# Three large loads merged into one DMA each over 128 partitions, and a list scheduler given measured durations

## The chip, the cores and the metric

The kernel runs on one core of one Trainium2 chip. The metric is the device time of one execution in microseconds (us). An execution is classed as slow when it takes over 1.5% more than the fastest of the same kernel.

Two words are used throughout. A *DMA engine* is one of the 16 units (the profile's page counts 16 for the core) that move data between HBM and the core's memory (SBUF). A *semaphore* is the counter that a load raises when its data has landed. The trace records these raises, and so shows when each load landed. The engines stand under short names in the views: TensorE (PE; PEld for its weight loads) does the matmuls, VectorE (DVE), ScalarE (ACT) and GpSimd (POOL) the rest of the arithmetic, and SyncE (SP) issues the loads. The span is the time from a program's first to its last instruction.

## The reference

Two layers are applied twice: a gated long convolution (A) and a small MLP (B), on a sequence of 2048 rows of 512.

```python
def _A_ref(q, k, v, shift_k, ssm_k, ssm_D):
    k_shift = sum over 4 taps of (k moved by t rows) * shift_k[:, tap]
    kv = k_shift * v
    y  = long convolution of kv with ssm_k (by FFT over 2*S) + kv * ssm_D
    return q * y
def _B_ref(x, w1, b1, w2, b2):
    return gelu(layernorm(x) @ w1 + b1) @ w2 + b2
# cut: types, padding, the FFT calls
x = A_q
x = x + _A_ref(layernorm(x), A_k, A_v, ...);  x = x + _B_ref(layernorm(x), ...)
x = x + _A_ref(layernorm(x), A_k, A_v, ...);  x = x + _B_ref(layernorm(x), ...)
```

The convolution result y does not depend on q. So the kernel computes y once, from k and v. Then it loads q, and the two layers follow.

## The kernel before

The program is built in three steps. Each operation is recorded with its reads, writes and an assumed duration. A list scheduler chooses engine and order from those durations. Then semaphore waits are put in. Every engine is given its own list, in that order.

```python
# P.op(engines, function, duration in ns, reads, writes, ...) records one operation
def dma(dst, src, nbytes, reads=(), prio=0.0, writes=None):          # all loads go through SyncE's queue
    return P.op(SP, lambda e: e.dma_start(dst, src, allow_slow_non_contiguous=True), 550.0, reads=reads,
                writes=[dst] if writes is None else writes, dma=True, nbytes=nbytes, prio=prio)
# A(p0, n, off, dims): n partitions of SBUF from p0;  dr(tensor, off, dims): HBM, dims = [step, count]
# ... cut: small tables, ssm_k (4 loads), shift_k
dma(A(64, 64, R_K, [1, 1536]), dr(A_k, 13 * 512, [32 * 512, 64], [1, 1536]), 3 << 16)     # three rows of halo
dma(A(1, 63, R_K, [1, 1536]), dr(A_k, 29 * 512, [32 * 512, 63], [1, 1536]), 3 << 16)
for g in range(2):
    dma(A(64 * g, 64, R_K + 1536, [1, 8192]), dr(A_k, 16 * g * 512, [32 * 512, 64], [1, 8192]), 1 << 20)
for g in range(2):
    dma(A(64 * g, 64, R_V, [1, 8192]), dr(A_v, 16 * g * 512, [32 * 512, 64], [1, 8192]), 1 << 20)
for j in range(8):
    tload(t_s2, 64 * 384, j * 3072, R_S2 + j * 3072, 3072)           # 6 MB of DFT tables, 128 partitions
# ... cut: transforms of ssm_k (PE, ACT)
def shift_chunk(w):                                                  # VectorE: taps of k, then times v
    # ... cut: three taps, adds, fourth tap, adds (7 operations of 128x2048)
    tt(..., A(0, 128, R_V + ...), ALU.mult, 610.0)                   # the first use of v, twice
    stage1(R_KP, ...)                                                # PE: first transform of kv
for w in range(4): shift_chunk(w)
products(0); products(1)                                             # VectorE: spectra times ssm_k's
inverse1(0); inverse1(1)
for g in range(2):                                                   # q, into memory that the spectra leave
    dma(A(64 * g, 64, R_X, [1, 8192]), dr(A_q, 16 * g * 512, [32 * 512, 64], [1, 8192]), 1 << 20)
# ... cut: second table, w1, w2, biases, then per layer and block: statistics of x, norms, MLP, residual
```

Partition p = 64g + c holds 16 consecutive rows of 512 from row 32c + 16g on. Each partition's data is one row of 16 KB in HBM. The 64 partitions of one half g take every second 16 KB row.

Of the kernel before, what the change touches and what calls it, by code (L numbers as in the profile page):

```python
# [7 lines left out]
ALU = mybir.AluOpType  # L8
AF = mybir.ActivationFunctionType
# [405 lines left out]
def bass_interleave_layers__ssm_conv_h3__mixer_channel_mlp__prompt_kernel(  # L415
        nc, A_q, A_k, A_v, A_shift_k, A_ssm_k, A_ssm_D, B_x, B_w1, B_b1, B_w2, B_b2, out):
    P = Prog(nc)
# [71 lines left out]
    dma(A(0, 128, R_SR, [1, 2048]), dr(A_shift_k, 0, [0, 128], [1, 2048]), 1 << 19)  # L489
    dma(A(64, 64, R_K, [1, 1536]), dr(A_k, 13 * 512, [32 * 512, 64], [1, 1536]), 3 << 16)  # L490
    dma(A(1, 63, R_K, [1, 1536]), dr(A_k, 29 * 512, [32 * 512, 63], [1, 1536]), 3 << 16)
    for g in range(2):
        dma(A(64 * g, 64, R_K + 1536, [1, 8192]), dr(A_k, 16 * g * 512, [32 * 512, 64], [1, 8192]), 1 << 20)
    for g in range(2):
        dma(A(64 * g, 64, R_V, [1, 8192]), dr(A_v, 16 * g * 512, [32 * 512, 64], [1, 8192]), 1 << 20)
    for j in range(8):
        tload(t_s2, 64 * 384, j * 3072, R_S2 + j * 3072, 3072)

# [9 lines left out]
    for a4 in range(4):  # L508
        tl = Tile(dconv)
        for al in range(4):  # L510
            ins = []
            for b in range(4):
                for g in range(2):
                    src = A(0, 128, R_HRAW + b * 2048 + 16 * g + 4 * a4 + al, [32, 64])
                    ins.append((g, al * 512 + b * 128, src))

            def f(e, ins=ins, tl=tl):
                for g, o, src in ins:
                    r = e.transpose(QB(tl, 64 * g, 64, o, [1, 128]), src, IDN)
                return r  # L520
            P.op(PE, f, 8 * 60.0, reads=[x[2] for x in ins] + [IDN], tile=tl)
        dst = A(0, 128, R_HP + 16 * a4, [4, 4], [64, 128], [1, 4])

        def f(e, dst=dst, tl=tl):
            src = QB(tl, 0, 128, 0, [512, 4], [4, 128], [1, 4])
            if e is nc.scalar:
                return e.activation(dst, src, AF.Copy)
            return e.tensor_copy(dst, src)
        P.op((ACT, DVE), f, {ACT: 2048 * .833 + 60, DVE: 2048 * .52 + 70}, writes=[dst], tile=tl)

    def stage1(src, G, gk, gh, dg0, n, engs, prio=0.0):


        for d8 in range(dg0 // 8, (dg0 + n) // 8):
            for h in range(2):
                tl = Tile(dconv)
                ins = [(64 * g, i, A(64 * g, 64, src + (64 * h + 8 * d8 + i) * 64, [1, 64]), A(64 * g, 64, R_F, [1, 128]))
                       for i in range(8) for g in range(2)]

                def f(e, ins=ins, tl=tl):  # L540
                    for p, i, w, m in ins:
                        r = e.matmul(Q(tl, p, 64, i * 128, [1, 128]), w, m, start=True, stop=True)  # L542
                    return r
                P.op(PE, f, 16 * 45.0, reads=[x for y in ins for x in y[2:]], tile=tl, prio=prio)
                dst = A(0, 128, G + gh(h, 8 * d8), [gk, 128], [1, 8])

                def f(e, dst=dst, tl=tl):
                    src = Q(tl, 0, 128, 0, [1, 128], [128, 8])
                    if e is nc.scalar:
                        return e.activation(dst, src, AF.Copy)  # L550
                    return e.tensor_copy(dst, src)
                P.op(engs, f, {ACT: 1100.0, DVE: 1024 * 1.04 + 90}, writes=[dst], tile=tl, prio=prio)

    def stage2(G, ks, n, pool, prio=0.0):

# [18 lines left out]
    for k4 in range(16):  # L574
        tl = stage2(R_GH, range(4 * k4, 4 * k4 + 4), 128, dconv, HP)
        dst = A(0, 128, R_H + k4 * 1024, [1, 1024])

        def f(e, dst=dst, tl=tl):
            src = Q(tl, 0, 128, 0, [1, 1024])
            if e is nc.scalar:  # L580
                return e.activation(dst, src, AF.Copy)  # L581
            return e.tensor_copy(dst, src)
        P.op((ACT, DVE), f, {ACT: 1024 * .833 + 60, DVE: 1024 * 1.04 + 70}, writes=[dst], tile=tl, prio=HP)


    def tt(o, a, b, op, dur, eng=DVE):
# [7 lines left out]
    def shift_chunk(w):  # L594

        tm = [A(0, 128, R_KP + w * 1024, [64, 16], [4096, 2], [1, 64])]
        tm += [A(0, 128, o, [128, 16], [64, 2], [1, 64]) for o in (R_TMP, R_TMP + 2048)]

        def tap(j, o):

            tt(o, A(0, 128, R_K + (3 - j) * 512 + w * 64, [512, 16], [256, 2], [1, 64]),
               A(0, 128, R_SJ[w] + j * 128, [0, 16], [64, 2], [1, 64]), ALU.mult, 1140.0)
        for j in range(3):
            tap(3 - j, tm[j])
        tt(tm[1], tm[0], tm[1], ALU.add, 1140.0)
        tap(0, tm[0])
        tt(tm[2], tm[1], tm[2], ALU.add, 1140.0)
        tt(tm[1], tm[2], tm[0], ALU.add, 1140.0)
        for h in range(2):
            tt(A(0, 128, R_KP + (64 * h + 16 * w) * 64, [4, 16], [64, 16], [1, 4]),  # L610
               A(0, 128, R_TMP + 64 * h, [128, 16], [4, 16], [1, 4]),
               A(0, 128, R_V + 256 * h + w * 64, [512, 16], [4, 16], [1, 4]), ALU.mult, 610.0)
        stage1(R_KP, R_GX + 8192 * (w // 2), 64, lambda h, dg: 32 * h + dg % 32, 16 * w, 16, EV_X)

    nx = [0]
# [1 line left out]
    def products(hf):  # L617

        for k8 in range(8):
# [5 lines left out]

            def f(e, xb=xb, tl=tl):
                return e.activation(xb, Q(tl, 0, 128, 0, [1, 1024]), AF.Copy)  # L627
            P.op(ACT, f, 1024 * .833 + 60, writes=[xb], tile=tl)
            ho = R_H + k8 * 2048 + 64 * hf
            x3 = A(0, 128, xo, [128, 8], [64, 2], [1, 64])  # L630
            tt(A(0, 128, po, [128, 8], [64, 2], [1, 64]), x3, A(0, 128, ho, [256, 8], [128, 2], [1, 64]), ALU.mult, 600.0)
            tt(x3, x3, A(0, 128, ho + 128, [256, 8], [-128, 2], [1, 64]), ALU.mult, 600.0)
            for ri, p in ((0, po), (1, xo)):
                tt(A(0, 128, R_Y + ri * 8192 + 8 * k8 * 64 + 32 * hf, [64, 8], [4096, 2], [1, 32]),
                   A(0, 128, p, [128, 8], [32, 2], [1, 32]), A(0, 128, p + 64, [128, 8], [32, 2], [1, 32]),
                   ALU.add if ri else ALU.subtract, 330.0)

    def inverse1(hf):

        for d4 in range(8 * hf, 8 * hf + 8):  # L640
# [14 lines left out]
            def f(e, dst=dst, tl=tl):  # L655
# [1 line left out]
                if e is nc.scalar:  # L657
                    return e.activation(dst, src, AF.Copy)  # L658
                return e.tensor_copy(dst, src)
            P.op((ACT, DVE), f, {ACT: 1024 * .833 + 60, DVE: 1024 * 1.04 + 70}, writes=[dst], tile=tl)  # L660

    for w in range(4):
        shift_chunk(w)
# [5 lines left out]


    tload(t_sm, row, 768, R_T2, 4096)
    for g in range(2):
        dma(A(64 * g, 64, R_X, [1, 8192]), dr(A_q, 16 * g * 512, [32 * 512, 64], [1, 8192]), 1 << 20)
    dma(A(0, 128, R_W1, [1376, 4], [1, 1376]), dr(B_w1, 0, [1376, 128], [128 * 1376, 4], [1, 1376]), 1409024)
    dma(A(0, 128, R_W2, [512, 10], [1, 512]), dr(B_w2, 0, [512, 128], [128 * 512, 10], [1, 512]), 1310720)
    dma(A(0, 96, R_W2 + 5120, [1, 512]), dr(B_w2, 1280 * 512, [512, 96], [1, 512]), 98304)
# [13 lines left out]
    for al2 in range(8):  # L690
# [18 lines left out]
        def f(e, dst=dst, tl=tl):  # L709
# [1 line left out]
            if e is nc.scalar:  # L711
                return e.activation(dst, src, AF.Copy)
            return e.tensor_copy(dst, src)
        P.op((ACT, DVE), f, {ACT: 1024 * .833 + 60, DVE: 1024 * 1.04 + 70}, writes=[dst], tile=tl)


    ptr, pm1, pm2 = Pool(1, 2), Pool(1, 3), Pool(1, 3)
# [2 lines left out]
    def stats(sl, double):  # L720
# [5 lines left out]
        for i, s in enumerate(sl):  # L726
            st = M(0, 128, M_ST + 6 * (4 * k + i), [1, 6])
            x = A(0, 128, R_X + s * 512, [1, 512])
            P.op(DVE, lambda e, st=st, x=x: e.bn_stats(st, x), 600.0, reads=[x], writes=[st])  # L729
            o = M(0, 128, mv + 2 * i, [1, 2])  # L730
            P.op(DVE, lambda e, st=st, o=o: e.bn_aggr(o, st), 100.0, reads=[st], writes=[o])
        v = M(0, 128, mv + 1, [2, n])
        r = M(0, 128, M_RS + 4 * k, [1, n])
        m1, a1 = (1.0 + EPS, EPS * EPS) if double else (1.0, EPS)
        P.op(POOL, lambda e: e.tensor_scalar(v, v, m1, a1, ALU.mult, ALU.add), 200.0, reads=[v], writes=[v])
        hf = M(0, 128, M_HF, [1, n])
        P.op(POOL, lambda e: e.tensor_tensor(r, v, hf, ALU.pow), 400.0, reads=[v, hf], writes=[r])  # L737
        return [(M(0, 128, mv + 2 * i, [1, 1]), M(0, 128, M_RS + 4 * k + i, [1, 1])) for i in range(n)]

    def norm(s, mr, o):  # L740
        x = A(0, 128, R_X + s * 512, [1, 512])
        m, r = mr
        P.op(DVE, lambda e: e.tensor_scalar(o, x, m, r, ALU.subtract, ALU.mult), 260.0, reads=[x, m, r], writes=[o])  # L743

    nn = [0]

# [6 lines left out]
    for L in range(2):  # L753
        for b in range(4):
            sl = list(range(4 * b, 4 * b + 4))
            mr = stats(sl, False)
            for i, s in enumerate(sl):
# [1 line left out]
                zt = A(0, 128, z, [1, 512])  # L759
                x = A(0, 128, R_X + s * 512, [1, 512])  # L760
                norm(s, mr[i], zt)
                tt(zt, zt, A(0, 128, R_YT + s * 512, [1, 512]), ALU.mult, 340.0)
                tt(x, x, zt, ALU.add, 340.0)
            mr = stats(sl, True)
            k = blk[0] % 2
            blk[0] += 1
            for i, s in enumerate(sl):
# [12 lines left out]
                def f(e, dst=dst, tl=tl):  # L780
# [1 line left out]
                    if e is nc.scalar:  # L782
                        return e.activation(dst, q, AF.Copy)  # L783
                    return e.tensor_copy(dst, q)
                P.op((ACT, DVE), f, {ACT: 490.0, DVE: 340.0}, writes=[dst], tile=tl)
            for fc in range(11):
                rows = 128 if fc < 10 else 96
                tl = Tile(pm1)
# [3 lines left out]
                def f(e, ins=ins, tl=tl, rows=rows):  # L792
# [4 lines left out]
                dst = A(0, rows, R_HT + k * 5632 + fc * 512, [1, 512])  # L797
                bias = M(0, rows, M_B1 + fc, [1, 1])
                P.op(ACT, lambda e, dst=dst, tl=tl, rows=rows, bias=bias: e.activation(  # L799
                    dst, Q(tl, 0, rows, 0, [1, 512]), AF.Gelu_apprx_tanh, bias=bias), 580.0,  # L800
                    reads=[bias], writes=[dst], tile=tl)
            for i, s in enumerate(sl):
                tl = Tile(pm2)
# [5 lines left out]
                for lo, hi in ((0, 4), (4, 8), (8, 11)):  # L809
                    def f(e, ins=ins, tl=tl, lo=lo, hi=hi):  # L810
# [2 lines left out]
                        return r  # L813
                    P.op(PE, f, (hi - lo) * 216.0, reads=[x for y in ins[lo:hi] for x in y], tile=tl)
                x = A(0, 128, R_X + s * 512, [1, 512])
                P.op(DVE, lambda e, x=x, tl=tl: e.tensor_tensor(x, x, Q(tl, 0, 128, 0, [1, 512]), ALU.add), 610.0,  # L816
                     reads=[x], writes=[x], tile=tl)
            if L == 1:
                for g in range(2):
# [34 lines left out]
```

## Time and profile before

| | before |
|---|---|
| time, median of 3 runs | 301.05 us (300.64 to 302.83) |
| span of the profiled run | 298.7 us |
| k landed / v landed / q landed | 24.0 / 34.6 / 93.8 us |
| first VectorE operation on k / on v | 24.07 / 35.43 us |

The landings are the last raises of each load's semaphore in the trace.

These are two lines from the part of the profile's page that follows the chain of work that ended last: shares of the span by engine, then by line.

```profile
PE 57%; DVE 20%; DMA 9%; ACT 7%; SPq 2%; POOL 2%; issue 1%
PE ps L794 25%; PE ps L812 24%; DVE ar L587 14%; DMA ar<-in_A_v_dram 9%; DVE sm L729 2%; PE ps L775 2%; ACT ar L658 2%; PE ps L566 2%; ACT ar L581 2%; SPq L470 2%; ACT ar L627 1%; POOL sm L737 1%; DVE ar L816 1%; ACT ar L550 1%; PE ps L650 1%
```

L794 and L812 are the MLP's matmuls, the second half of the kernel. Ahead of them stand VectorE (DVE), whose shift chunks and products are L587, and the load of v. The next view, of one source line, says when the MLP runs. The line is the weight loads of L794; the two times after the durations are the first and the last start.

```profile
L794 PEld LDWEIGHTS ps<-ar x352: 95/98/151, 131.1 to 273.8; 128*128 128x128 bf16 x160, 128*96 128x96 bf16 x16
```

VectorE's timeline (start, length, operation, count, and in brackets the idle time before it and what ended it):

```profile
15.85 2.38 DVE L528 COPY ar<-ps 128x2048 bf16<-128x2048 bf16 x2 [2.75 <-PE ps L519]
24.07 38.17 DVE L587 TENSOR_TENSOR ar<-ar 128x2048 bf16<-128x2048 bf16 x36 [5.84 <-DMA ar<-in_A_k_dram]
...
102.33 1.28 DVE L729 BATCH_NORM_STATS2 sm<-ar 128x6 f32<-128x512 bf16 x2
```

VectorE waits 5.84 us for k and then works through 36 operations without a pause. The single operations in the trace show that the eleventh, at 35.43 us, is the first that reads v, 0.8 us after v has landed. The layer-norm statistics of q start at 102.33 us, when q has been there for 8 us.

SyncE's queue, which issues the loads (start, time until the last of the group was issued):

```profile
4.38 2.32 SPq L470 DMA_DIRECT2D ar<-in_A_k_dram  x4
6.74 1.25 SPq L470 DMA_DIRECT2D ar<-in_A_v_dram  x2
8.03 10.84 SPq L478 DMA_DIRECT2D ar<-tab_s  x8
...
79.77 1.27 SPq L470 DMA_DIRECT2D ar<-in_A_q_dram  x2
```

The busy times in two stretches follow. The last three columns are the granted TensorE clock, the mean busy share of the 16 DMA engines, and the rate in GB/s. The engines come first in each row, with the count of instructions in brackets.

```profile
core 0: us, PE busy (x) PEld busy (x) DVE busy (x) ACT busy (x) POOL busy (x), PEclk, DMA share, GB/s
15.00:30.00 15.00, 10.23 (x232) 9.12 (x229) 8.31 (x8) 12.56 (x12) 0.00 (x0) 0.89 1.00 210
36.00:48.00 12.00, 8.87 (x192) 7.18 (x192) 11.83 (x13) 10.10 (x11) 0.00 (x0) 0.81 1.02 416
```

The first stretch carries k and v in halves of 64 partitions, the second the tables over 128. All engines are busy in both, but in the first they move half as much. A 16 KB row took about 1.25 us there. A 6 KB row of the tables took 0.236 us, at which rate 16 KB would take 0.63.

### The profile page before, as it was taken

The numbers are of one execution on the slowest core, as the hardware profiler recorded it, in microseconds if no ns is written. First come the engines' busy times: TensorE is split into PE (matmuls) and PEld (weight loads), VectorE is DVE, ScalarE is ACT, GpSimd is POOL, SyncE is SP. The second block draws the span as 40 slices with busy tenths as digits, with TensorE's granted clock in tenths as the row PEclk, the third lists the DMA queues.
The fourth block names the chain that finished last, engine by engine and source line by source line (L and its number), as shares of the span: only waits on it lengthen the run. The fifth ranks groups of instructions, "written<-read, shape, count | busy, mean of one in ns | idle before, by whom it ended". The sixth has DMA issues, their size and how long they took to land.

```text
span 298.7 us, 5389 instructions
## 1 busy us (share of the span) xinstructions
PE 247.2 (83%) x2304; PEld 145.5 (49%) x2304; DVE 194.8 (65%) x409; ACT 153.8 (51%) x196; POOL 25.7 (9%) x43
## 2 busy tenths in 40 slices
PE   0667175899899386169999999999999999999993
PEld 0666155788889284133444534444434444434441
DVE  0137999989999999899687775866995111201132
ACT  1069097689968299245445264454468502373100
POOL 2000000300010031213011011030021000000000
PEclk9989779799999899669999999999999999999998
DMA  6999996000199600000000000000000000200222
GB/s 203 295 211 211 278 414 214 2 20 3 37 224 324 193 27 2 1 2 0 0 2 0 0 1 2 0 0 2 0 0 3 0 0 2 70 0 0 72 70 70
DMA packets 7473, 22.10 MB, mean 74 GB/s; under 512 B 2490, under 2 KB 4123, under 8 KB 6938
## 3 DMA queue, kind: packets, MB, share of 16 engines
q1 hardware_dynamic: 7450, 21.76, 25.7%
q8 instruction: 18, 0.29, 0.4%
q14 instruction: 5, 0.04, 0.0%
HBM read 19.66 MB, written 2.10 MB: 73 GB/s over the span
## 4 chain that ended last, share of the span: by engine, by line
PE 57%; DVE 20%; DMA 9%; ACT 7%; SPq 2%; POOL 2%; issue 1%
PE ps L794 25%; PE ps L812 24%; DVE ar L587 14%; DMA ar<-in_A_v_dram 9%; DVE sm L729 2%; PE ps L775 2%; ACT ar L658 2%; PE ps L566 2%; ACT ar L581 2%; SPq L470 2%; ACT ar L627 1%; POOL sm L737 1%; DVE ar L816 1%; ACT ar L550 1%; PE ps L650 1%
## 5 line engine op out<-in xcount | busy, mean ns | idle before, releaser
L587 DVE TENSOR_TENSOR ar<-ar 128x512 bf16<-128x512 bf16 (+2 forms) x164 | 92.7, 620 | 7.2 <-DMA ar<-in_A_k_dram 5.8
L799 ACT ACTIVATE ar<-ps,sm 128x512 bf16<-128x512 f32 (+1 forms) x88 | 59.4, 687 | 53.0 <-PE ps L794 29.3
L794 PE MATMUL ps<-ar 128*128 128x512 bf16 (+1 forms) x352 | 82.4, 383 | 0.0
L812 PE MATMUL ps<-ar 128*128 128x512 bf16 (+1 forms) x352 | 79.6, 379 | 0.0
L794 PEld LDWEIGHTS ps<-ar 128*128 128x128 bf16 (+1 forms) x352 | 31.1, 101 | 46.8 <-ACT ar L799 17.8
L812 PEld LDWEIGHTS ps<-ar 128*128 128x128 bf16 (+1 forms) x352 | 33.2, 98 | 40.5 <-ACT ar L799 3.2
L816 DVE TENSOR_TENSOR ar<-ar,ps 128x512 bf16<-128x512 bf16 x32 | 21.0, 682 | 47.4 <-PE ps L812 47.4
L729 DVE BATCH_NORM_STATS2 sm<-ar 128x6 f32<-128x512 bf16 x64 | 41.8, 681 | 0.4
L743 DVE TENSOR_SCALAR ar<-ar,sm 128x512 bf16<-128x512 bf16 x64 | 23.6, 407 | 23.0 <-POOL sm L737 12.1
L550 ACT ACTIVATE ar<-ps 128x1024 bf16<-128x1024 f32 x32 | 30.0, 1048 | 11.5 <-PE ps L542 11.5
L542 PE MATMUL ps<-ar 64*64 64x128 bf16 x512 | 21.3, 241 | 16.4 <-DVE ar L587 9.7
L566 PE MATMUL ps<-ar 128*128 128x128 bf16 (+1 forms) x192 | 31.4, 244 | 2.1 <-ACT ar L550 1.5
L568 PE MATMUL ps<-ar 128*128 128x64 bf16 (+1 forms) x192 | 29.9, 206 | 0.0
L567 PE MATMUL ps<-ar 128*128 128x64 bf16 (+1 forms) x192 | 29.9, 205 | 0.0
L783 ACT ACTIVATE ar<-ps 128x512 bf16<-128x512 bf16 x24 | 13.4, 594 | 31.5 <-PE ps L775 31.2
L542 PEld LDWEIGHTS ps<-ar 64*64 64x64 bf16 x512 | 18.0, 122 | 19.6 <-issue 7.2
L650 PE MATMUL ps<-ar 128*128 128x256 bf16 x128 | 16.8, 292 | 5.5 <-DVE ar L587 5.2
L566 PEld LDWEIGHTS ps<-ar 128*128 128x128 bf16 x192 | 19.1, 100 | 3.9 <-ACT ar L550 1.8
L775 PE MATMUL ps<-ar 128*128 128x128 bf16 x128 | 11.5, 236 | 10.2 <-DVE ar L743 10.2
L568 PEld LDWEIGHTS ps<-ar 128*128 128x128 bf16 x192 | 19.2, 100 | 1.2
L567 PEld LDWEIGHTS ps<-ar 128*128 128x128 bf16 x192 | 19.2, 100 | 0.0
L650 PEld LDWEIGHTS ps<-ar 128*128 128x128 bf16 x128 | 15.2, 175 | 6.6 <-DVE ar L587 5.6
(28 smaller groups left out, 135.4 us busy)
## 6 DMA issues: line engine op xcount, KB each, us to landing
ar<-tab_s SPq DMA_DIRECT2D x8, 768.0 KB, 33.9
ar<-in_A_ssm_k_dram SPq DMA_DIRECT2D x4, 512.0 KB, 5.3
ar<-in_A_k_dram SPq DMA_DIRECT2D x2, 1024.0 KB, 15.7
ar<-in_A_v_dram SPq DMA_DIRECT2D x2, 1024.0 KB, 24.8
ar<-in_A_q_dram SPq DMA_DIRECT2D x2, 1024.0 KB, 10.6
out_dram<-ar SPq DMA_DIRECT2D x8, 256.0 KB, 3.1
ar<-in_B_w_dram SPq DMA_DIRECT2D x1, 1376.0 KB, 8.5
ar<-in_B_w_dram SPq DMA_DIRECT2D x1, 1280.0 KB, 6.1
```

Of the source, the lines that this page charges most:

```text
L542: r = e.matmul(Q(tl, p, 64, i * 128, [1, 128]), w, m, start=True, stop=True)
L550: return e.activation(dst, src, AF.Copy)
L566: e.matmul(Q(tl, 0, 128, i * 2 * n, [1, 2 * n]), t[0], gg[0], start=True, stop=False)
L567: e.matmul(Q(tl, 0, 128, i * 2 * n, [1, n]), t[1], gg[1], start=False, stop=False)
L568: r = e.matmul(Q(tl, 0, 128, i * 2 * n + n, [1, n]), t[2], gg[2], start=False, stop=True)
L587: return P.op(eng, lambda e: e.tensor_tensor(o, a, b, op), dur, reads=[a, b], writes=[o])
L650: r = e.matmul(Q(tl, 0, 128, i * 256, [1, 256]), w, m, start=ri == 0, stop=ri == 1)
L729: P.op(DVE, lambda e, st=st, x=x: e.bn_stats(st, x), 600.0, reads=[x], writes=[st])
L794: r = e.matmul(Q(tl, 0, rows, 0, [1, 512]), w, m, start=dk == 0, stop=dk == 3)
L799: P.op(ACT, lambda e, dst=dst, tl=tl, rows=rows, bias=bias: e.activation(dst, Q(tl, 0, rows, 0, [1, 512]), AF.Gelu_apprx_tanh, bias=bias), ...
L812: r = e.matmul(Q(tl, 0, 128, 0, [1, 512]), ins[fc][0], ins[fc][1], start=fc == 0, stop=fc == 10)
L816: P.op(DVE, lambda e, x=x, tl=tl: e.tensor_tensor(x, x, Q(tl, 0, 128, 0, [1, 512]), ALU.add), 610.0, reads=[x], writes=[x], tile=tl)
```

## The change

The intent is to lift that 210 GB/s. Each of k, v and q is loaded by one DMA over all 128 partitions, as the tables are. Besides, the scheduler gets the durations that the profile shows. The diff's core:

```diff
-    for g in range(2):
-        dma(A(64 * g, 64, R_K + 1536, [1, 8192]), dr(A_k, 16 * g * 512, [32 * 512, 64], [1, 8192]), 1 << 20)
-    for g in range(2):
-        dma(A(64 * g, 64, R_V, [1, 8192]), dr(A_v, 16 * g * 512, [32 * 512, 64], [1, 8192]), 1 << 20)
+    dma(A(0, 128, R_K + 1536, [1, 8192]), dr(A_k, 0, [16 * 512, 2], [32 * 512, 64], [1, 8192]), 1 << 21)
+    dma(A(0, 128, R_V, [1, 8192]), dr(A_v, 0, [16 * 512, 2], [32 * 512, 64], [1, 8192]), 1 << 21)
@@ the same for q @@
@@ durations, a selection of those changed @@
-        P.op((ACT, DVE), f, {ACT: 1024 * .833 + 60, DVE: 1024 * 1.04 + 70}, writes=[dst], tile=tl, prio=HP)
+        P.op((ACT, DVE), f, {ACT: 1045.0, DVE: 1217.0}, writes=[dst], tile=tl, prio=HP)
-        P.op(POOL, lambda e: e.tensor_tensor(r, v, hf, ALU.pow), 400.0, reads=[v, hf], writes=[r])
+        P.op(POOL, lambda e: e.tensor_tensor(r, v, hf, ALU.pow), 1050.0, reads=[v, hf], writes=[r])
```

Partition 64g + c is to take the row of 16 KB number 2c + g. One pattern over the 128 partitions must therefore count g outermost: the source becomes [2][64][8192] elements, while the destination stays [128][8192].

More of the change, by code (lines that the diff above doesn't have):

```diff
@@ L528, in f @@
             return e.tensor_copy(dst, src)
-        P.op((ACT, DVE), f, {ACT: 2048 * .833 + 60, DVE: 2048 * .52 + 70}, writes=[dst], tile=tl)
+        P.op((ACT, DVE), f, {ACT: 1870.0, DVE: 1225.0}, writes=[dst], tile=tl)
     def stage1(src, G, gk, gh, dg0, n, engs, prio=0.0):
@@ L543, in f @@
                     return r
-                P.op(PE, f, 16 * 45.0, reads=[x for y in ins for x in y[2:]], tile=tl, prio=prio)
+                P.op(PE, f, 16 * 41.0, reads=[x for y in ins for x in y[2:]], tile=tl, prio=prio)
                 dst = A(0, 128, G + gh(h, 8 * d8), [gk, 128], [1, 8])
@@ L551, in f @@
                     return e.tensor_copy(dst, src)
-                P.op(engs, f, {ACT: 1100.0, DVE: 1024 * 1.04 + 90}, writes=[dst], tile=tl, prio=prio)
+                P.op(engs, f, {ACT: 1050.0, DVE: 1217.0}, writes=[dst], tile=tl, prio=prio)
     def stage2(G, ks, n, pool, prio=0.0):
@@ L601, in tap @@
             tt(o, A(0, 128, R_K + (3 - j) * 512 + w * 64, [512, 16], [256, 2], [1, 64]),
-               A(0, 128, R_SJ[w] + j * 128, [0, 16], [64, 2], [1, 64]), ALU.mult, 1140.0)
+               A(0, 128, R_SJ[w] + j * 128, [0, 16], [64, 2], [1, 64]), ALU.mult, 1220.0)
         for j in range(3):
             tap(3 - j, tm[j])
-        tt(tm[1], tm[0], tm[1], ALU.add, 1140.0)
+        tt(tm[1], tm[0], tm[1], ALU.add, 1220.0)
         tap(0, tm[0])
-        tt(tm[2], tm[1], tm[2], ALU.add, 1140.0)
-        tt(tm[1], tm[2], tm[0], ALU.add, 1140.0)
+        tt(tm[2], tm[1], tm[2], ALU.add, 1220.0)
+        tt(tm[1], tm[2], tm[0], ALU.add, 1220.0)
         for h in range(2):
@@ L611, in shift_chunk @@
                A(0, 128, R_TMP + 64 * h, [128, 16], [4, 16], [1, 4]),
-               A(0, 128, R_V + 256 * h + w * 64, [512, 16], [4, 16], [1, 4]), ALU.mult, 610.0)
+               A(0, 128, R_V + 256 * h + w * 64, [512, 16], [4, 16], [1, 4]), ALU.mult, 690.0)
         stage1(R_KP, R_GX + 8192 * (w // 2), 64, lambda h, dg: 32 * h + dg % 32, 16 * w, 16, EV_X)
@@ L627, in f @@
                 return e.activation(xb, Q(tl, 0, 128, 0, [1, 1024]), AF.Copy)
-            P.op(ACT, f, 1024 * .833 + 60, writes=[xb], tile=tl)
+            P.op(ACT, f, 1045.0, writes=[xb], tile=tl)
             ho = R_H + k8 * 2048 + 64 * hf
             x3 = A(0, 128, xo, [128, 8], [64, 2], [1, 64])
-            tt(A(0, 128, po, [128, 8], [64, 2], [1, 64]), x3, A(0, 128, ho, [256, 8], [128, 2], [1, 64]), ALU.mult, 600.0)
-            tt(x3, x3, A(0, 128, ho + 128, [256, 8], [-128, 2], [1, 64]), ALU.mult, 600.0)
+            tt(A(0, 128, po, [128, 8], [64, 2], [1, 64]), x3, A(0, 128, ho, [256, 8], [128, 2], [1, 64]), ALU.mult, 690.0)
+            tt(x3, x3, A(0, 128, ho + 128, [256, 8], [-128, 2], [1, 64]), ALU.mult, 690.0)
             for ri, p in ((0, po), (1, xo)):
@@ L635, in products @@
                    A(0, 128, p, [128, 8], [32, 2], [1, 32]), A(0, 128, p + 64, [128, 8], [32, 2], [1, 32]),
-                   ALU.add if ri else ALU.subtract, 330.0)
+                   ALU.add if ri else ALU.subtract, 420.0)
     def inverse1(hf):
@@ L659, in f @@
                 return e.tensor_copy(dst, src)
-            P.op((ACT, DVE), f, {ACT: 1024 * .833 + 60, DVE: 1024 * 1.04 + 70}, writes=[dst], tile=tl)
+            P.op((ACT, DVE), f, {ACT: 1045.0, DVE: 1217.0}, writes=[dst], tile=tl)
     for w in range(4):
@@ L671, in bass_interleave_layers__ssm_conv_h3__mixer_channel_mlp__prompt_kernel @@
     tload(t_sm, row, 768, R_T2, 4096)
-    for g in range(2):
-        dma(A(64 * g, 64, R_X, [1, 8192]), dr(A_q, 16 * g * 512, [32 * 512, 64], [1, 8192]), 1 << 20)
+    dma(A(0, 128, R_X, [1, 8192]), dr(A_q, 0, [16 * 512, 2], [32 * 512, 64], [1, 8192]), 1 << 21)
     dma(A(0, 128, R_W1, [1376, 4], [1, 1376]), dr(B_w1, 0, [1376, 128], [128 * 1376, 4], [1, 1376]), 1409024)
@@ L713, in f @@
             return e.tensor_copy(dst, src)
-        P.op((ACT, DVE), f, {ACT: 1024 * .833 + 60, DVE: 1024 * 1.04 + 70}, writes=[dst], tile=tl)
+        P.op((ACT, DVE), f, {ACT: 1045.0, DVE: 1217.0}, writes=[dst], tile=tl)
     ptr, pm1, pm2 = Pool(1, 2), Pool(1, 3), Pool(1, 3)
@@ L728, in stats @@
             x = A(0, 128, R_X + s * 512, [1, 512])
-            P.op(DVE, lambda e, st=st, x=x: e.bn_stats(st, x), 600.0, reads=[x], writes=[st])
+            P.op(DVE, lambda e, st=st, x=x: e.bn_stats(st, x), 640.0, reads=[x], writes=[st])
             o = M(0, 128, mv + 2 * i, [1, 2])
-            P.op(DVE, lambda e, st=st, o=o: e.bn_aggr(o, st), 100.0, reads=[st], writes=[o])
+            P.op(DVE, lambda e, st=st, o=o: e.bn_aggr(o, st), 140.0, reads=[st], writes=[o])
         v = M(0, 128, mv + 1, [2, n])
@@ L742, in norm @@
         m, r = mr
-        P.op(DVE, lambda e: e.tensor_scalar(o, x, m, r, ALU.subtract, ALU.mult), 260.0, reads=[x, m, r], writes=[o])
+        P.op(DVE, lambda e: e.tensor_scalar(o, x, m, r, ALU.subtract, ALU.mult), 400.0, reads=[x, m, r], writes=[o])
     nn = [0]
@@ L761, in bass_interleave_layers__ssm_conv_h3__mixer_channel_mlp__prompt_kernel @@
                 norm(s, mr[i], zt)
-                tt(zt, zt, A(0, 128, R_YT + s * 512, [1, 512]), ALU.mult, 340.0)
-                tt(x, x, zt, ALU.add, 340.0)
+                tt(zt, zt, A(0, 128, R_YT + s * 512, [1, 512]), ALU.mult, 420.0)
+                tt(x, x, zt, ALU.add, 420.0)
             mr = stats(sl, True)
@@ L784, in f @@
                     return e.tensor_copy(dst, q)
-                P.op((ACT, DVE), f, {ACT: 490.0, DVE: 340.0}, writes=[dst], tile=tl)
+                P.op((ACT, DVE), f, {ACT: 595.0, DVE: 420.0}, writes=[dst], tile=tl)
             for fc in range(11):
@@ L799, in bass_interleave_layers__ssm_conv_h3__mixer_channel_mlp__prompt_kernel @@
                 P.op(ACT, lambda e, dst=dst, tl=tl, rows=rows, bias=bias: e.activation(
-                    dst, Q(tl, 0, rows, 0, [1, 512]), AF.Gelu_apprx_tanh, bias=bias), 580.0,
+                    dst, Q(tl, 0, rows, 0, [1, 512]), AF.Gelu_apprx_tanh, bias=bias), 690.0,
                     reads=[bias], writes=[dst], tile=tl)
@@ L815, in bass_interleave_layers__ssm_conv_h3__mixer_channel_mlp__prompt_kernel @@
                 x = A(0, 128, R_X + s * 512, [1, 512])
-                P.op(DVE, lambda e, x=x, tl=tl: e.tensor_tensor(x, x, Q(tl, 0, 128, 0, [1, 512]), ALU.add), 610.0,
+                P.op(DVE, lambda e, x=x, tl=tl: e.tensor_tensor(x, x, Q(tl, 0, 128, 0, [1, 512]), ALU.add), 685.0,
                      reads=[x], writes=[x], tile=tl)
```

## The prediction

> **What bounds the kernel now (298.7 us span).** Two halves. From about 131 us to the end the chain of waits is nearly all TensorE matmuls of the MLP (L794 and L812, half of the span). Before that, VectorE: in the timeline it runs the shift chunks without a gap from 24.07 (k has landed) to 62.2 us, and stays over 90% busy to 113 us. Its first product with v starts at 35.43 us, just after v has landed (last semaphore event 34.6; the chain of waits gives 27.0 us, 9%, to that load). The loads of k and v run at 210 GB/s with the DMA engines fully busy (stretches 15 to 30 us); the table load after them, over 128 partitions, runs at 417 GB/s (35 to 48 us). So the intent: a half load wastes half of the rate.
>
> **What the change does.** It removes three DMA issues (0.6 us each, hidden), and gives the scheduler mostly longer DVE and ACT durations and a POOL pow of 1050 instead of 400 ns (1060 in the trace). The arithmetic stays. I give the new order -4 to +4 us.
>
> **The step that decides: how many DMA engines the new load uses.** The source becomes [2][64][8192], the destination [128][8192]. [...] the 63-partition halo load of k shows nine separate late semaphore events and one early (63 = 9 x 7), the one-row load of b2 one and one, all 64- and 128-partition loads sixteen. [...] One engine moves 4096 B in 159 ns and 6144 B in 236 ns here, 26 GB/s; a 16 KB row is then 0.63 us, and 64 rows per engine are 40 us per 2 MB load (estimate), against about 10 us now.
>
> - k starts at about 13.5 us, lands at 54 (now 24). v lands at 94.6 (now 34.6). The first product with v moves from 35.4 to 94.7: +59 us, on the critical path.
> - q is issued at 79.8 + 59 = 139 and lands at about 180 (now 94). The layer-norm statistics (now at 102.3, then 162) wait until 180; twelve us of them stand before the first product with YT, now at 114.15, then at 192: +78 in all. The second table, behind q in the queue, lands at 183 and delays the last transform less than that.
>
> **Predicted: 379 us**, range 352 to 425. Faster by over 2%: 0.14 (the load spreads over 16 engines: v 10 us and k 5 us earlier, about 293 us). Within 2%: 0.04. Slower by over 2%: 0.82.
>
> **What would show it.** DMA share near 0.12 and about 52 GB/s in long stretches, one from 14 to 95 us and one of 40 us for q; the k load landing about 45 us after issue, v over 80; VectorE idle about 29 us for k, 30 for v and 18 for q; the MLP's stretch unchanged. Against it: 400 GB/s between 12 and 22 us.
>
> **What would make it wrong.** The program may carry the source in another form, so that all engines work. A 16 KB row may not reach 26 GB/s on a lone engine[...]; then it is far slower. The new order may put statistics ahead of products, so that the wait for q blocks more.

The counts of semaphore events led to two engines per merged load, and the sum rests on those two: 64 rows of 0.63 us on each are 40 us per load, and with three such loads the delays come to +78 us on 301, the 379 us predicted.

## The result

| | before | after |
|---|---|---|
| time, median (runs) | 301.94 us (4, 300.64 to 304.11) | 396.20 us (4, 395.41 to 396.88) |
| ratio of fast runs | | 1.3111, 95% interval 1.3022 to 1.3201 |
| span of the profiled run | 298.7 us | 394.3 us |
| k / v / q landed | 24.0 / 34.6 / 93.8 us | 54.2 / 104.0 / 193.4 us |
| raises per load of k, v, q | 16 late ones per half | 1 early, 2 late |

A ratio here is the mean time of one kernel's fast runs over that of the other's of the same rounds, so it is not quite the ratio of the medians.

The result is correct, and 94 us slower. The semaphore of each merged load is raised once at issue and only twice more, when the data has landed. Two engines carried it: the DMA share was 0.13, two of sixteen, while k landed (below).

The chain of the changed kernel, by engine and by line:

```profile
PE 46%; DMA 24%; DVE 11%; another core or an unknown queue 10%; ACT 4%; SPq 1%; issue 1%; POOL 1%; DVEq 0%
PE ps L791 19%; PE ps L809 19%; DMA ar<-in_A_k_dram 12%; DMA ar<-in_A_q_dram 12%; DVE ar L585 7%; DVE sm L726 2%; PE ps L648 2%; PE ps L772 2%; PE ps L564 2%; ACT ar L579 2%; ACT ar L625 1%; ACT ar L548 1%; SPq L470 1%; PE ps L540 1%
```

The loads of k and q have taken 12% of the span each. The 10% of "an unknown queue" stand in the chain from 65.62 to 104.04 us. Here is that piece, and after it the list of waits, which names what was waited for there, v:

```profile
65.62 38.42 another core or an unknown queue
```

```profile
DVE ar L585 <- DMA ar<-in_A_v_dram: 38.5, 1, 38.5
DVE ar L585 <- DMA ar<-in_A_k_dram: 35.4, 1, 35.4
DVE sm L726 <- DMA ar<-in_A_q_dram: 30.8, 1, 30.8
```

Line numbers are two or three lower than before, since lines went out above them. VectorE's timeline:

```profile
54.17 11.45 DVE L585 TENSOR_TENSOR ar<-ar 128x2048 bf16<-128x2048 bf16 x10 [35.37 <-DMA ar<-in_A_k_dram]
104.13 13.34 DVE L585 TENSOR_TENSOR ar<-ar 128x1024 bf16<-128x1024 bf16 x13 [38.51 <-DMA ar<-in_A_v_dram]
...
193.47 0.69 DVE L726 BATCH_NORM_STATS2 sm<-ar 128x6 f32<-128x512 bf16 x1 [30.82 <-DMA ar<-in_A_q_dram]
194.07 5.09 DVE L585 TENSOR_TENSOR ar<-ar 128x512 bf16<-128x512 bf16 x11
```

After the ten operations that need only k, VectorE stands until v is there. It stands again for q. Eleven operations of the products now come behind the first statistic, a consequence of the new order. The issues on SyncE's queue:

```profile
4.36 1.93 SPq L470 DMA_DIRECT2D ar<-in_A_k_dram  x3
6.34 2.63 SPq L470 DMA_DIRECT2D ar<-in_A_v_dram  x1
9.01 85.90 SPq L478 DMA_DIRECT2D ar<-tab_s  x8
...
146.19 0.52 SPq L470 DMA_DIRECT2D ar<-in_A_q_dram  x1
```

The eight table loads behind k and v needed 85.90 us to be issued instead of 10.84; in a later run (e8), where they stand ahead of the merged k and v, it took 3.71. The stretches of the loads (k; v with tables; the end of q):

```profile
14.00:46.00 32.00, 12.27 (x276) 11.16 (x274) 2.39 (x2) 13.83 (x13) 0.00 (x0) 0.72 0.13 54
50.00:95.00 45.00, 0.00 (x0) 0.00 (x0) 11.45 (x10) 0.00 (x0) 0.00 (x0) 0.50 0.45 138
168.00:193.00 25.00, 0.00 (x0) 0.00 (x0) 0.00 (x0) 0.00 (x0) 0.00 (x0) 0.50 0.13 53
```

A share of 0.13 is two of sixteen engines, and 53 GB/s is 27 per engine. In the middle stretch the other engines move tables: of the first seven table loads, 14 of the 16 raises each came by 93.9 us and the other two only from 99.9 on, after the first late raise of v (98.2). TensorE's mean granted clock fell from 0.951 to 0.826, but not in the MLP, where it is 0.99 in both kernels. It is 0.50 in the two of these stretches that have no matmul (0.00 in the first column). So the fall goes with the waiting. The MLP itself:

```profile
L791 PEld LDWEIGHTS ps<-ar x352: 95/98/151, 229.5 to 368.5; 128*128 128x128 bf16 x160, 128*96 128x96 bf16 x16
```

The sum over milestones, from the numbers above:

| milestone | before | after | later by |
|---|---|---|---|
| first product with v | 35.4 | 104.1 | 68.7 |
| q issued | 79.8 | 146.2 | 66.4 |
| first statistic of q | 102.3 | 193.5 | 91.1 |
| MLP's first weight load | 131.1 | 229.5 | 98.4 |
| end of the span | 298.7 | 394.3 | 95.6 |

### The profile page after: what moved, and what is told of

Same layout as the page of the kernel before. It is cut to its first block, busy times and chain, and to the rows that moved or that the text cites. A ratio compares the mean times of both kernels' runs of the same rounds, so it can differ in the third digit from the quotient of the medians.

```text
span 394.3 us, 5380 instructions
## 1 busy us (share of the span) xinstructions
PE 244.2 (62%) x2287; PEld 152.2 (39%) x2304; DVE 191.6 (49%) x405; ACT 155.8 (40%) x200; POOL 24.8 (6%) x43
## 4 chain that ended last, share of the span: by engine, by line
PE 46%; DMA 24%; DVE 11%; another core or an unknown queue 10%; ACT 4%; SPq 1%; issue 1%; POOL 1%; DVEq 0%
PE ps L791 19%; PE ps L809 19%; DMA ar<-in_A_k_dram 12%; DMA ar<-in_A_q_dram 12%; DVE ar L585 7%; DVE sm L726 2%; PE ps L648 2%; PE ps L772 2%; PE ps L564 2%; ACT ar L579 2%; ACT ar L625 1%; ACT ar L548 1%; SPq L470 1%; PE ps L540 1%
## 5 line engine op out<-in xcount | busy, mean ns | idle before, releaser
L585 DVE TENSOR_TENSOR ar<-ar 128x512 bf16<-128x512 bf16 (+2 forms) x164 | 92.2, 621 | 76.9 <-DMA ar<-in_A_v_dram 38.5
L796 ACT ACTIVATE ar<-ps,sm 128x512 bf16<-128x512 f32 (+1 forms) x88 | 59.3, 687 | 54.6 <-PE ps L791 27.3
L809 PE MATMUL ps<-ar 128*128 128x512 bf16 (+1 forms) x345 | 78.8, 379 | 0.4
L791 PE MATMUL ps<-ar 128*128 128x512 bf16 (+1 forms) x342 | 78.4, 383 | 0.9 <-ACT ar L780 0.5
L540 PE MATMUL ps<-ar 64*64 64x128 bf16 x512 | 24.0, 261 | 81.5 <-DVE ar L585 75.9
L548 ACT ACTIVATE ar<-ps 128x1024 bf16<-128x1024 f32 x32 | 30.4, 1058 | 76.1 <-PE ps L540 76.1
L726 DVE BATCH_NORM_STATS2 sm<-ar 128x6 f32<-128x512 bf16 x64 | 41.5, 683 | 31.1 <-DMA ar<-in_A_q_dram 30.8
L540 PEld LDWEIGHTS ps<-ar 64*64 64x64 bf16 x512 | 20.5, 135 | 84.5 <-issue 74.8
L791 PEld LDWEIGHTS ps<-ar 128*128 128x128 bf16 (+1 forms) x352 | 35.2, 101 | 40.1 <-issue 1.1
L809 PEld LDWEIGHTS ps<-ar 128*128 128x128 bf16 (+1 forms) x352 | 33.9, 98 | 39.0
L740 DVE TENSOR_SCALAR ar<-ar,sm 128x512 bf16<-128x512 bf16 x64 | 23.6, 406 | 18.1 <-PE ps L772 15.1
L564 PE MATMUL ps<-ar 128*128 128x128 bf16 (+1 forms) x192 | 30.0, 238 | 2.1 <-ACT ar L579 1.1
L648 PEld LDWEIGHTS ps<-ar 128*128 128x128 bf16 x128 | 15.2, 175 | 36.8 <-DVE ar L585 35.9
L565 PE MATMUL ps<-ar 128*128 128x64 bf16 (+1 forms) x192 | 29.2, 202 | 0.0
L566 PE MATMUL ps<-ar 128*128 128x64 bf16 (+1 forms) x192 | 29.2, 202 | 0.0
L656 ACT ACTIVATE ar<-ps 128x1024 bf16<-128x1024 f32 x13 | 12.9, 1034 | 36.6 <-PE ps L648 36.4
L780 ACT ACTIVATE ar<-ps 128x512 bf16<-128x512 bf16 x27 | 15.2, 595 | 27.5 <-PE ps L772 27.3
L564 PEld LDWEIGHTS ps<-ar 128*128 128x128 bf16 x192 | 18.8, 98 | 4.0 <-ACT ar L579 2.0
L566 PEld LDWEIGHTS ps<-ar 128*128 128x128 bf16 x192 | 18.8, 98 | 0.7
```

Source lines behind the costliest of these rows:

```text
L540: r = e.matmul(Q(tl, p, 64, i * 128, [1, 128]), w, m, start=True, stop=True)
L548: return e.activation(dst, src, AF.Copy)
L564: e.matmul(Q(tl, 0, 128, i * 2 * n, [1, 2 * n]), t[0], gg[0], start=True, stop=False)
L565: e.matmul(Q(tl, 0, 128, i * 2 * n, [1, n]), t[1], gg[1], start=False, stop=False)
L566: r = e.matmul(Q(tl, 0, 128, i * 2 * n + n, [1, n]), t[2], gg[2], start=False, stop=True)
L585: return P.op(eng, lambda e: e.tensor_tensor(o, a, b, op), dur, reads=[a, b], writes=[o])
```

## The experiments

My theory had two parts. The first: the merged loads run on two DMA engines because their source has 2 outermost, and the lost engines cost the 94 us. The second, formed while reading the result: the partitions to which the steps of a load go matter as well. That was a guess: the runs show rates that differ with the order of the partitions, not the cause. The rivals: large or three-dimensional loads are slow by themselves; the new order costs a good part; 16 KB rows are slow for a reason on the HBM side. Twelve kernels ran; their kernels of before, on the same chips, took 300.99 to 301.74 us (medians). Where a result is wrong on purpose, only the rows that land in a partition differ, not the bytes moved.

### The merged loads alone: e2_merge_only

Edit: the six lines of the diff above that concern k, v and q; the old durations.

> The three merged loads alone, old durations and so the old order of instructions. Theory: the loads on two DMA engines account for nearly all of the loss: v lands at about 104 us, the first product with v moves from 35.4 to 104 (+69), q is issued at about 148 and lands 47 us later, at 195, the twelve us of statistics follow: about 394 us (388 to 399). Rival: a good part of the loss beyond the predicted 379 us comes from the new order (a statistic put ahead of eleven products): then about 380 us.

Measured: 396.22 us, ratio 1.3148 (1.3083 to 1.3213). With the loads alone the whole loss is there; the new durations have no net part in it. Its VectorE timeline at q, and the weight loads of its MLP:

```profile
197.14 1.29 DVE L726 BATCH_NORM_STATS2 sm<-ar 128x6 f32<-128x512 bf16 x2 [28.10 <-DMA ar<-in_A_q_dram]
```

```profile
L791 PEld LDWEIGHTS ps<-ar x352: 95/98/152, 225.3 to 369.0; 128*128 128x128 bf16 x160, 128*96 128x96 bf16 x16
```

From the first statistic to the MLP it takes 28.2 us (225.3 - 197.1), as before (131.1 - 102.3 = 28.8). In the changed kernel that stretch takes 36.0 us (229.5 - 193.5), but q lands 3.7 us earlier, and the MLP takes 164.8 us instead of 168.7 (span less its start; the span of this run is 394.0). So the new kernel loses some 8 us in one place and gets them back in two others. The durations, and with them the order, are all that differs between the two; whether q's earlier landing comes from it, one profile of each cannot say.

### q alone: e3_q_merged

Edit: only the q load is merged.

> Only q is merged; k and v stay in halves. Theory: q is issued at 79.8 as before and lands 47 us later, at about 127 instead of 94; the statistics start at 127 instead of 102.3 us, so the kernel takes about 25 us more: 326 us (320 to 332). If the q load had slack enough to hide (rival: only k and v matter), about 301 us.

Measured: 327.38 us, ratio 1.0880 (1.0809 to 1.0951). Its VectorE timeline at q:

```profile
129.66 1.29 DVE L728 BATCH_NORM_STATS2 sm<-ar 128x6 f32<-128x512 bf16 x2 [27.24 <-DMA ar<-in_A_q_dram]
```

VectorE waits 27.24 us for q and begins its statistics at 129.66 us, 27.3 us later than before. The merged q thus costs 26 us by itself, because only 8 us lay between its landing and its use. The expectation held.

### Four engines: e4_source_4 (wrong result)

Edit, on top of e2_merge_only, for k, v and q:

```diff
-dr(A_k, 0, [16 * 512, 2], [32 * 512, 64], [1, 8192])
+dr(A_k, 0, [16 * 512, 4], [4 * 16 * 512, 32], [1, 8192])
```

> Wrong result on purpose: the merged loads with the same 2 MB and the same 128 destination partitions, but the source walked as [4][32] rows instead of [2][64], so that rows land on other partitions. Theory[...]: four engines, four late landings of the semaphore; 32 rows of 0.61 us per engine = 20 us per load; k lands at about 32, v at about 53, q about 23 us after its issue; about 323 us (315 to 332). Rival (a single load of 2 MB, or a source of three dimensions, is slow by itself): as with [2][64], about 394 us.

Measured: 375.20 us, ratio 1.2471 (1.2394 to 1.2548). Both theory and rival missed. The count is as the theory says: each load's semaphore has four late raises. But k landed at 54.1 us, exactly as with two engines, and a row took 1.21 us (median of the k, v and q rows) instead of 0.61. For k, four engines at half the speed are worth two. (v then took 32.0 us instead of 49.9, hence most of the 21 us between this kernel and the changed one; why v went faster than k was not tested.) So the count of engines is not all. VectorE's timeline at k and v:

```profile
54.10 11.44 DVE L585 TENSOR_TENSOR ar<-ar 128x2048 bf16<-128x2048 bf16 x10 [35.80 <-DMA ar<-in_A_k_dram]
86.19 24.25 DVE L585 TENSOR_TENSOR ar<-ar 128x1024 bf16<-128x1024 bf16 x23 [20.64 <-DMA ar<-in_A_v_dram]
```

What held the four back is not in the trace. My guess was the partitions they write: the outermost steps of this source go to partitions 32 apart, those of the change to partitions 64 apart. The following runs vary that layout.

### Sixteen engines: e4_source_16 (wrong result)

```diff
-dr(A_k, 0, [16 * 512, 2], [32 * 512, 64], [1, 8192])
+dr(A_k, 0, [16 * 512, 16], [16 * 16 * 512, 8], [1, 8192])
```

> Wrong result on purpose: the same, with the source walked as [16][8] rows. Theory: sixteen engines over all 128 partitions, the load that the change wanted: 410 GB/s, about 5 us per load; k lands at about 18 and v at about 23 us; VectorE starts its shift chunks near 18.3 instead of 24.1 us and the kernel is about 5.5 us faster than before: 295.5 us (292 to 299). Rival (a single load of 2 MB or a source of three dimensions is slow by itself): about 394 us.

Measured: 300.38 us, ratio 0.9965 (0.9914 to 1.0015): the same as before. Each load has sixteen late raises; yet k landed at 23.2 and v at 32.9 us instead of the expected 18 and 23, and a row took 1.25 us. A stretch with k and v (busy times by engine, clock, DMA share and GB/s, as above):

```profile
15.00:30.00 15.00, 10.10 (x232) 9.16 (x230) 9.12 (x8) 12.92 (x12) 0.00 (x0) 0.89 0.99 211
```

Sixteen engines over all 128 partitions, all of them busy (0.99), move 211 GB/s, which is the rate of the halves. That answers the first rival: a single load of 2 MB with a source of three dimensions is not slow as such, since it does as well as two halves. It also shows that 128 partitions and sixteen engines together are not enough for 410 GB/s.

### 128 outermost on both sides: e9_source_128 (wrong result)

```diff
-dr(A_k, 0, [16 * 512, 2], [32 * 512, 64], [1, 8192])
+dr(A_k, 0, [16 * 512, 128], [1, 8192])
```

> Wrong result on purpose: the merged loads with old durations, the source walked as 128 plain rows, so that both sides have 128 outermost. In the run with [16][8] sixteen engines over 128 partitions still took 10 us per load. Theory: [...]as for the tables: 400 GB/s, k lands at 18, v at 23 us, about 295.5 us (292 to 299). Rival: rows of 16 KB are slow whenever sixteen engines read them (1.25 us each): v lands at 33 us, 300 us.

Measured: 296.38 us, ratio 0.9822 (0.9783 to 0.9861). Two stretches of it in the same view, the first within k and v, the second of the tables:

```profile
15.00:20.00 5.00, 2.19 (x40) 2.06 (x38) 4.10 (x4) 3.65 (x2) 0.00 (x0) 1.00 0.98 413
25.00:30.00 5.00, 3.12 (x80) 2.31 (x80) 5.00 (x6) 5.00 (x6) 0.00 (x0) 1.00 1.01 410
```

k landed at 17.9 and v at 23.6 us; a row took 0.61 us with sixteen engines at work. So rows of 16 KB are not slow as such. This is the load that the change wanted, and it is worth 5 us (clear of zero; the interval reaches across 2%). Which partition each engine took is not in the trace, so why the [16][8] walk moves 211 GB/s and the [128] walk 413, with sixteen engines busy in both, is not shown.

### Two engines, outermost steps 32 partitions apart: e10_two_engines_half and e12_half_tables_first (wrong results)

Edit, on top of the kernel before, for k, v and q (in the second run the tables are also issued ahead of k and v):

```diff
-dr(A_k, 16 * g * 512, [32 * 512, 64], [1, 8192])
+dr(A_k, 64 * g * 16 * 512, [16 * 512, 2], [32 * 512, 32], [1, 8192])
```

The source is walked in two outermost steps over every second row of 16 KB, as in the change, and two engines are at work, as in the change (share 0.13). A load is now a half, and the destination differs: 64 partitions, so that the two outermost steps go to partitions 32 apart.

> Wrong result on purpose: loads in halves of 64 partitions, the source of each half walked as [2][32] rows, so two engines per load[...]. Theory[...]: the two engines get half a rate each, 1.22 us a row instead of 0.61: k lands at 91, v near 170 us, about 495 us (470 to 520). Rival (the four-engine run was slow for another reason, such as what the memory on the source side gives): 0.61 us a row, v near 104, about 396 us.

> Wrong result on purpose: halves of 64 partitions on two engines as in the run before, with the eight table loads issued ahead of k and v. There the first half load took 39 us[...], and the next ones 26 us; tables ran beside those. Theory: the tables on the other engines knocked the two out of step[...]; with the tables gone by 29 us every half of k and v takes 39 us: k lands near 107, v near 185 us, some 510 us in all. Rival: the two fall out of step by themselves after the first load: halves of about 26 us from the second on, v near 147 us, some 440 us in all.

Measured: e10 took 423.36 us in its one fast run and 431.11 in a slow one. Its profile is of the slow run, so nothing rests on it alone. In it the loads of k and v took 39, 26, 26 and 25 us (landing to landing, the first from its first row on), neither 39 throughout nor 20. e12 took 426.54 us, ratio 1.4069 (1.3978 to 1.4159), with a fast profile. Its halves landed at 65.1, 91.3, 111.1 and 130.7 us. Stretches of the first, the second and the third half:

```profile
29.00:40.00 11.00, 6.98 (x95) 5.67 (x96) 0.00 (x0) 8.34 (x10) 0.00 (x0) 0.75 0.13 28
...
70.00:90.00 20.00, 0.00 (x0) 0.00 (x0) 0.00 (x0) 0.00 (x0) 0.00 (x0) 0.50 0.13 43
95.00:115.00 20.00, 0.00 (x0) 0.00 (x0) 7.79 (x7) 0.00 (x0) 0.00 (x0) 0.50 0.13 54
```

The share of 0.13 says that two engines are at work all the time. They move 28, then 43, then 54 GB/s. In the first half they are held to half of what the change's two engines moved from the start (54), although they read in the same steps, and the third half, of the same size, moved 54. So I take the brake to be on the destination side; what it is there, no trace shows. Then the brake wears off. My expectation of 510 us was wrong, since it took the brake for permanent; in e12 no table load is left to disturb the two engines, so the rival was right that they fall out of step by themselves. In e12 their last raises for the first half are already 0.8 us apart (64.3 and 65.1 us). The rest can be read from the single 16 KB rows in the same trace (its DMA records; no view prints them). At first the two engines start their rows within 0.1 us of each other, and nearly every row takes 0.95 to 1.3 us. As one engine falls behind, fewer and fewer of each four successive rows are slow, and the others take 0.61 us: at a distance of 1.3 us about two of four, at 2.0 us one or two. From the 73rd row on one engine is 2.31 us behind, nearly four rows of 0.61 us, and every row takes 0.61 us to the end of v. So in this trace the row time went with the distance. No run set the distance on purpose; why it matters and why one engine falls behind stay open.

### The new durations alone: e1_durations_only

Edit: the diff without its loads.

> The new durations alone, loads in halves as before. Theory: they are worth little, within 4 us either way: 297 to 305 us. Rival: the new order is itself a loss of some 15 us, which would explain why the change measured 396 and not 379 us: 315 us.

Measured: 299.15 us, ratio 0.9916 (0.9883 to 0.9950), within 2% but clear of zero. The MLP starts 1.3 us later than before (132.4 us) and takes 165.5 us instead of 167.6 (spans 297.9 and 298.7, less the start). It is the fastest correct kernel, by 0.8%. The rival, that the order costs 15 us, is out.

### The tables ahead of k and v: e8_tables_first

Edit, on top of the changed kernel: the loop of eight table loads moves up, ahead of the two merged loads.

> The changed kernel with the eight table loads issued ahead of k and v. Theory: v took 50 us and not 40 because the tables on the other fourteen engines compete with the two that carry v. With the tables gone by 27 us, k lands at about 67 and v 40 us after it, at 108; about 400 us. Rival: v's load takes 50 us by itself: v lands at 117 us and the kernel takes 409 us or more.

Measured: 396.85 us (2 runs), ratio 1.3161 (1.3093 to 1.3229). k landed at 67.6 and v at 106.7 us, 39 us later. In the changed kernel that difference was 49.9 us. A stretch of v's load:

```profile
68.00:106.00 38.00, 0.00 (x0) 0.00 (x0) 11.02 (x10) 0.00 (x0) 0.00 (x0) 0.50 0.13 53
```

The two engines keep 53 GB/s throughout when no tables run beside them. So the tables did cost v 10 us. The single rows agree. In the changed kernel 33 of v's 128 rows took over 0.7 us, in bursts at the times when tables were on the move; they make the later of the two engines 10.8 us longer. In e8 no row of v did. The time as a whole stays, because k now starts behind them.

### Halves on two queues: e6_two_queues, e7_two_queues_durations, e11_two_queues_late

A half moved 210 GB/s, the tables over 128 partitions 416; that two halves at once might reach the latter was my estimate. Edit for k and v (the loads of q stay; e7 and e11 have the new durations):

```diff
-    dma(A(64 * g, 64, R_V, [1, 8192]), dr(A_v, 16 * g * 512, [32 * 512, 64], [1, 8192]), 1 << 20)
+    dma(A(64 * g, 64, R_V, [1, 8192]), dr(A_v, 16 * g * 512, [32 * 512, 64], [1, 8192]), 1 << 20, eng=(SP, ACT)[g])
@@ e11 only: ScalarE's halves wait for the last ssm_k load (hr is that load) @@
+    ... eng=(SP, ACT)[g], after=((), (hr,))[g])
```

> Loads in halves and old durations, but the halves for partitions 64 to 127 of k and v are issued from ScalarE's queue instead of SyncE's, so that both halves are under way at once. Theory: a half load is held at 210 GB/s[...]; two halves at once reach some 400 GB/s; v lands near 22 instead of 34.6 us, VectorE starts the shift chunks at 17 to 19 instead of 24.1 us: 295 us (292 to 299). Rival[...]: v lands at 34 us as before, 301 us.

> The same with the new durations as well. If the two are independent, the time of the run before this, plus what the durations alone give: 290 to 301 us.

> New durations, loads in halves, the halves for partitions 64 to 127 of k and v on ScalarE's queue, but issued only when the last ssm_k load has landed, so that they do not run ahead of the first loads, which cost the earlier two-queue runs 10 us at the start. Theory: [...]two at once reach some 400 GB/s; k lands near 18 and v near 23 us; 293 us (290 to 297). Rival: [...]nothing is gained: v lands at 34 us, 299 us.

Measured: 310.96 us, ratio 1.0307 (1.0271 to 1.0344); 303.75 us, ratio 1.0067 (1.0033 to 1.0101); 313.05 us, ratio 1.0388 (1.0354 to 1.0422). All three expectations failed, and two of the kernels are slower. In e6 and e7 the design was at fault: ScalarE's halves, with nothing to wait for, ran ahead of the first loads (issued at 0.73 and 1.30 us in e6). In e6 shift_k landed at 21.3 us instead of 11.6, and the halves never ran side by side. e11 mends that; in it both queues are at work together:

```profile
15.00:20.00 5.00, 2.17 (x40) 2.04 (x38) 2.36 (x2) 3.65 (x2) 0.00 (x0) 1.00 1.00 213
20.00:25.00 5.00, 4.99 (x120) 4.91 (x122) 0.00 (x0) 4.31 (x5) 0.00 (x0) 0.66 1.06 252
```

213 and 252 GB/s, so hardly any gain: k was complete at 28.8 us, v at 35.2. The rival of that run was right about the loads (v at 34 us), but not about the time (299 us). Besides, with the halves of v under way beside it, k lands 5 us later than before (28.8 instead of 24.0). e11 takes 13.9 us more than e1, the same durations with one queue. VectorE's timelines tell where, first of e11, then of e1:

```profile
28.77 14.92 DVE L587 TENSOR_TENSOR ar<-ar 128x2048 bf16<-128x2048 bf16 x14 [10.54 <-DMA ar<-in_A_k_dram]
50.38 1.22 DVE L582 CAST ar<-ps 128x1024 bf16<-128x1024 f32 x1 [6.68 <-PE ps L568]
51.52 1.22 DVE L587 TENSOR_TENSOR ar<-ar 128x2048 bf16<-128x2048 bf16 x1
55.83 1.23 DVE L582 CAST ar<-ps 128x1024 bf16<-128x1024 f32 x1 [3.10 <-PE ps L568]
...
24.20 24.69 DVE L587 TENSOR_TENSOR ar<-ar 128x2048 bf16<-128x2048 bf16 x23 [5.88 <-DMA ar<-in_A_k_dram]
49.46 1.23 DVE L582 CAST ar<-ps 128x1024 bf16<-128x1024 f32 x1 [0.57 <-PE ps L568]
```

k comes 4.6 us later. Besides, the scheduler put two casts into the midst of the chunks, where VectorE stands 6.68 and 3.10 us for TensorE. So most of e11's loss is its order, and its time says little about the two queues; the rates above do.

## Why the prediction was right

**The step that decides: right.** Two engines per merged load were predicted. The semaphores show two late raises per merged load, and four and sixteen where the source's outermost dimension was 4 and 16. The late raises counted: 63 partitions: 9; 1: 1; 64 or 128 on both sides: 16; 2 against 128: 2; 4 against 128: 4; 16 against 128: 16.

**The engine's rate: right.** 0.63 us per row was estimated, 0.61 measured; k was predicted to land at 54 us and landed at 54.2.

**v: mis-sized.** "v lands at 94.6": it landed at 104.0. The step that failed is the term of 40 us for v's load. It took 49.9 us from k's landing, since the table loads, queued behind v, run on the other engines at the same time. e8 takes them away and measures 39. So +68.7 instead of +59 us for the first product. The prediction had the two engines alone at work until 95 us; in truth the others moved tables beside v (share 0.45, 138 GB/s).

**q: mis-sized.** "issued at 79.8 + 59 = 139 and lands at about 180": issued at 146.2, landed at 193.4, so 47 us after its issue instead of 41. The second table and w1, queued behind it, share its first 19 us (DMA share 0.57 from 146 to 168 us); the trace shows 27 of q's rows there at over 0.7 us (up to 1.29), and all at 0.61 afterwards. No run took those loads away, so for q the cause is carried over from v. VectorE's waits were longer to match: 35.4, 38.5 and 30.8 us where 29, 30 and 18 were predicted.

v and q together put the first statistic at 193.5 us instead of 180, which is 13 of the 17 us between 379 and 396. The other 4 came after q: the way from the first statistic to the MLP took 7.2 us more than before, and the MLP 2.8 less.

**The new order: right in sum.** -4 to +4 us was predicted. Alone it measured 0.8% faster, and beside the merged loads it came to nothing (396.22 without, 396.20 with). That its parts cancel there, some 8 us lost and as many gained, was luck: the prediction named only the loss, and as a risk. The fear that statistics would stand ahead of products came true for one statistic. It cost time there that came back elsewhere.

**The MLP unchanged: right**, 167.6 and 164.8 us.

**A step that was wrong and did no harm:** the alternative. "The load spreads over 16 engines: v 10 us and k 5 us earlier, about 293 us." e4_source_16 spreads over sixteen engines and gains nothing (300.38 us). Only with 128 outermost on both sides (e9) was it 296.4 us.

The intent failed, then, where a pattern had to count the two halves outermost. The layout puts row 2c + g on partition 64g + c; any one load over 128 partitions in this order has a 2 outermost on the HBM side. What remains open: a correct load of k and v at 410 GB/s with this layout. The halves on two queues were not it.

## What to carry to other kernels

Before you merge DMAs, look at the outermost dimension on both sides, and count the late raises of the semaphore afterwards: here the merge that made one of them 2 left two of sixteen engines (two late raises, share 0.13, 53 GB/s). If the count is right and the rate is still half, try another order of the partitions: with sixteen engines busy, [16][8] moved 211 GB/s here and [128] 413. The DMA share (busy) beside the GB/s tells such a load from one on few engines. And ask what is queued behind a load that becomes slow: here it waited, and it also slowed the load down (v took 49.9 us with the tables behind it and 39 without).
